# Weight conversion at the start of a top-k attention kernel: the size of each weight written whole to SBUF and multiplied by eight on GpSimd, in place of halves in PSUM that VectorE shifts

## The chip, the cores and the metric

The kernel runs on one core of one Trainium2 chip. The metric is the device time of one execution in microseconds (us); below, "before" is the kernel as it stood and "after" the changed one. The engines are called TensorE (PE in the profile; PEld is its weight load), VectorE (DVE), ScalarE (ACT), GpSimd (POOL) and SyncE (SP), whose queue here issues all DMAs.

## What is computed

Attention that keeps the 32 largest scores of each row, over 8 batches, 8 heads, 576 positions and 64 channels, and behind it a mixer over the positions and channels of each batch:

```python
scores = scale * np.matmul(q, k.transpose(0, 1, 3, 2))
kth = np.partition(scores, -top_k, axis=-1)[..., -top_k:-top_k + 1]
scores = np.where(scores >= kth, scores, -1000000000.0)
attn = np.exp(scores - np.max(scores, axis=-1, keepdims=True))
x = attn / (np.sum(attn, axis=-1, keepdims=True) + 1e-09) @ v      # heads side by side: (8, 576, 512)

theta = x @ w_theta
yr = np.einsum('ts,bsd->btd', w_tok_r, x * np.cos(theta))
yi = np.einsum('ts,bsd->btd', w_tok_i, x * np.sin(theta))
u = x + yr + yi
out = u + np.maximum(u @ w_ch, 0.0)
```

The four weights come as 64-bit floats. The kernel makes 32-bit floats of them itself, and the change is in that step.

## The kernel before

**Work units.** A unit is one tile of 128 query rows of two heads (a pair); each pair has four full units and a half one for the last 64 rows, so a batch has 4 pairs of 5 units and the kernel has 160 units, here counted from 0. A unit goes through these steps. TensorE makes its scores (`ps_score`, from `q2`, `kh`, `kl`). ScalarE copies one part of them to SBUF (`e<-ps_score`). VectorE folds them into a short list (`fold`, `pick`: the tensor_tensor lines on `ps_score`, `lo`, `lst`, and the max lines that write `lst`), finds the 32nd largest in four rounds of max and match_replace (`threshold`), and ends with a small reduce on `best`, called the closing reduce below. GpSimd makes the limit (`lim`), ScalarE a penalty (`pen`), GpSimd subtracts it (`e<-e,pen`, called the subtract below), ScalarE takes the exponent in place, TensorE transposes (`pt`) and multiplies with the values (`px`).

**Mixer.** When a batch is through, its mixer runs piece by piece beside the units of the next batches; the last batch's mixer runs alone at the end.

**Loads of a pair.** `load_pair` fetches `raw`; ScalarE casts it to `hi`, GpSimd makes `raw - hi`, and twelve DMAs lay both out as `q2`, `kh`, `kl` before TensorE can make the first scores of the pair. Pair 0 has a shorter way of its own (`twice`).

**Weights.** `widen_steps` holds 17 conversion jobs: 4 tiles of `w_theta` (128 x 512), 9 of the two token weights (128 x 576), 4 of `w_ch` (128 x 512). A job reads both halves of the 64-bit words by DMA into one of two buffers (`raws`; the DMA of a job waits until the job two before it is through). ScalarE scales the low word into `low`, takes the magnitude of the high word times 2^-112 as a float, and takes its sign in place. The magnitude's bit pattern, shifted left by three, is the bit pattern of the 32-bit float but for its last bits; GpSimd adds `low`, and multiplies by the sign. All of `raws` and `tmps` is one tile, `room`, in the profile. The step "M" of the unit loop emits one job per unit.

**Order.** Code order gives priorities; a scheduler puts all instructions into one queue per engine before the run, with a timeline of its own. Each queue is then worked through strictly in order. So a change of one step can reorder all five queues. Buffers tie the engines together: 11 tiles `e` (also used by `raw` and `hi`), 4 `lst`, 4 `best`, 3 `lim`, 2 score tiles in PSUM.

Of the kernel before, what the change touches and what calls it, by code (L numbers as in the profile page):

```python
# [9 lines left out]
F32 = mybir.dt.float32  # L10
F32R = mybir.dt.float32r
BF16 = mybir.dt.bfloat16
I32 = mybir.dt.int32
U32 = mybir.dt.uint32
AF = mybir.ActivationFunctionType
ALU = mybir.AluOpType
AX = mybir.AxisListType

P = 128
# [27 lines left out]
def topk_attention_phase_mixer(  # L47
# [11 lines left out]
    nc = tc.nc  # L59
    B, NPAIR, _, S = qT.shape  # L60
    DM = w_ch.shape[0]
# [18 lines left out]
    const = ctx.enter_context(tc.tile_pool(name="const", bufs=1))  # L80
# [5 lines left out]
    ps_m = ctx.enter_context(tc.tile_pool(name="ps_m", bufs=2, space=bass.MemoryType.PSUM))  # L86
# [3 lines left out]
    nc.vector.memset(magic, MAGIC)  # L90
    half_pi = const.tile([P, 1], F32, name="half_pi")
    nc.vector.memset(half_pi, HALF_PI)
    warm = const.tile([P, 1], F32, name="warm")
    nc.scalar.activation(warm, magic, AF.Exp, scale=0.0)
    make_identity(nc, ident)
# [20 lines left out]
    def weight_tile(dtype, width):  # L116
        if width == S:
            return wk2.tile([P, S], dtype, tag="w", name="w", bufs=KB + 1)
        return wk2.tile([P, DM], dtype, tag="w5", name="w5", bufs=2 * NB)

    def widen_steps():
        for key, n, width in (("ch", NB, DM), ("th", NB, DM), ("tok", KB, S)):
            wts[key] = [weight_tile(F32, width) for _ in range(n)]
        jobs = []
        for c in range(NB):
            jobs.append((wts["th"][c], (w_theta[c * P : c * P + P],), INV_TWO_PI))
        toks = (w_tok_r, w_tok_i)
        for i, w in enumerate(toks):
            for c in range(NJ):
                jobs.append((wts["tok"][i * NJ + c], (w[c * P : c * P + P],), None))  # L130
        jobs.append((wts["tok"][2 * NJ], [w[NJ * P :] for w in toks], None))
        for c in range(NB):
            jobs.append((wts["ch"][c], (w_ch[c * P : c * P + P],), None))

        room = one.tile([P, ZB * DM], I32, tag="z", name="room")
        raws = [room[:, i * 2 * S : (i + 1) * 2 * S].rearrange("p (n t) -> p n t", t=2) for i in range(2)]
        tmps = [room[:, (i + 2) * 2 * S : (i + 3) * 2 * S].rearrange("p (t n) -> p t n", t=2) for i in range(2)]

        def fetch(i):
            dst, srcs, _ = jobs[i]  # L140
            n = P // len(srcs)
            for k, src in enumerate(srcs):
                nc.sync.dma_start(
                    raws[i % 2][k * n : k * n + n, : dst.shape[-1]],
                    src.bitcast(I32).rearrange("p (n t) -> p n t", t=2),
                )

        def convert(i):
            dst, _, factor = jobs[i]
            n = dst.shape[-1]  # L150
            word, tail = raws[i % 2][:, :n, 1], raws[i % 2][:, :n, 0]
            bits, low = tmps[i % 2][:, 0, :n], tmps[i % 2][:, 1, :n]
            sign = word.bitcast(F32)
            nc.scalar.activation(low, tail.bitcast(U32), AF.Copy, scale=2.0**-29)
            m = n if n <= DM else n // 2
            for c in range(0, n, m):
                size = ps_m.tile([P, 512], F32, tag="m", name="size")[:, :m]
                nc.scalar.activation(size, sign[:, c : c + m], AF.Abs, scale=2.0**-112)
                nc.vector.tensor_scalar(bits[:, c : c + m], size.bitcast(I32), 3, None, op0=ALU.logical_shift_left)
            nc.scalar.activation(sign, sign, AF.Sign)  # L160
            nc.gpsimd.tensor_add(low, low, bits)
            nc.gpsimd.tensor_mul(dst, low.bitcast(F32), sign)
            if factor is not None:
                nc.scalar.mul(dst, dst, factor)

        fetch(0)
        for _ in range(WSTART):
            yield
        for i in range(len(jobs)):
            if i + 1 < len(jobs):  # L170
                fetch(i + 1)
            convert(i)
            yield
# [696 lines left out]
```

## Time and profile before

| | |
|---|---|
| median of 3 runs | 1235.96 us (1234.65 to 1238.25) |
| the profiled execution | 1236.12 us, span 1234.2 us |
| TensorE busy | 1134.4 us, 92% of the span |
| VectorE busy | 1114.9 us, 90% |
| ScalarE busy | 1014.9 us, 82% |
| GpSimd busy | 683.6 us, 55% |
| mean granted TensorE clock | 0.963 |

Busy shares are means over stages with different limits. The weight conversion lies in the first 164 us, in which 20 to 21 of the 160 units and no mixer run.

### The profile page before, as it was taken

What the parts mean: (1) busy time and instruction counts of PE and PEld (TensorE: products, weight loads), DVE (VectorE), ACT (ScalarE), POOL (GpSimd) and SP (SyncE); (2) the same over time, 40 slices, a digit from 0 to 9 for tenths busy, and PEclk for the clock granted to TensorE, in tenths of its full rate; (3) what the DMA queues carried; (4) which work ended last, traced back from release to release, by engine and by line L of the source; (5) the groups of instructions that cost most, each with busy time, mean ns of one, the idle gap of its engine ahead of it and who ended that gap; (6) DMA issues with size and microseconds to landing.
All of it is one profiled execution on the core that took longest, in us unless ns stands there. A gap on an engine that the chain in (4) does not pass through costs nothing.

```text
span 1234.2 us, 22874 instructions
## 1 busy us (share of the span) xinstructions
PE 1134.4 (92%) x6293; PEld 845.6 (69%) x6293; DVE 1114.9 (90%) x5018; ACT 1014.9 (82%) x2098; POOL 683.6 (55%) x958
## 2 busy tenths in 40 slices
PE   4676689799989999999989999999999999999998
PEld 3554456577757876677757777677856777677688
DVE  7999999899999999999999899999999999995353
ACT  4799998998799987898788987898788987888361
POOL 2678873855356553766354654656455654657240
PEclk9776789899999999999999999999999999999999
DMA  6544533333423244333421334233322334200101
GB/s 162 131 131 142 157 90 85 86 87 78 118 64 77 59 107 107 78 90 83 126 63 53 87 97 117 68 96 78 108 68 76 87 97 116 68 19 2 39 2 41
DMA packets 71016, 106.11 MB, mean 86 GB/s; under 512 B 13920, under 2 KB 32608, under 8 KB 70880
## 3 DMA queue, kind: packets, MB, share of 16 engines
q1 hardware_dynamic: 70880, 104.57, 31.9%
q8 instruction: 52, 0.85, 0.3%
q14 instruction: 84, 0.69, 0.2%
HBM read 38.40 MB, written 9.44 MB: 39 GB/s over the span
## 4 chain that ended last, share of the span: by engine, by line
PE 49%; DVE 27%; ACT 16%; issue 3%; DMA 3%; POOL 2%; SPq 1%; ACTq 0%; DVEq 0%; POOLq 0%
PE py L656 18%; PE ps_score L261 7%; PE px L408 7%; PE pt L378 6%; DVE lst L327 5%; DVE best L321 5%; DVE lst L305 5%; PE pth L539 4%; PE po L683 4%; ACT e L363 3%; ACT pen L351 3%; DVE lo L298 3%; ACT e L270 2%; DVE ps_score L297 2%; DVE lst L299 2%
## 5 line engine op out<-in xcount | busy, mean ns | idle before, releaser
L353 POOL TENSOR_TENSOR e<-e,pen 128x576 f32<-128x576 f32 x288 | 365.6, 1284 | 140.0 <-ACT pen L351 137.0
L321 DVE MAX8 best<-lst 128x8 f32<-128x102 f32 (+3 forms) x1152 | 294.5, 310 | 10.8 <-POOL lim L332 10.3
L656 PE MATMUL py<-w,z 128*128 128x288 f32 x1008 | 267.3, 408 | 0.3 <-ACT xt L420 0.3
L363 ACT ACTIVATE e<-e,lim 128x576 f32<-128x576 f32 x288 | 225.0, 782 | 22.3 <-POOL e L353 21.7
L327 DVE MATCH_REPLACE8 lst<-best,lst 128x102 f32<-128x102 f32 (+2 forms) x864 | 241.1, 297 | 0.3 <-issue 0.3
L351 ACT ACTIVATE pen<-e,lim 128x576 bf16<-128x576 f32 x288 | 210.3, 775 | 13.4 <-POOL lim L332 12.9
L305 DVE MAX8 lst<-lo 128x8 f32<-128x72 f32 (+1 forms) x864 | 217.5, 315 | 0.1
L261 PE MATMUL ps_score<-kh,q 128*128 128x288 f32 x512 | 185.0, 376 | 31.0 <-ACT e L270 13.6
L656 PEld LDWEIGHTS py<-w,z 128*128 128x128 f32 x1008 | 182.6, 191 | 40.9 <-ACT xt L420 1.2
L378 PE MATMUL pt<-ident,e 128*128 128x128 f32 x1152 | 183.2, 284 | 26.6 <-ACT e L363 18.8
L378 PEld LDWEIGHTS pt<-ident,e 128*128 128x128 f32 x1152 | 141.7, 145 | 68.6 <-ACT e L363 24.0
L270 ACT COPY e<-ps_score 128x576 f32<-128x576 f32 x256 | 162.1, 641 | 29.4 <-PE ps_score L261 28.1
L380 ACT COPY at<-pt 128x512 f32<-128x512 f32 x256 | 149.7, 588 | 29.3 <-PE pt L378 28.8
L408 PE MATMUL px<-at,vt 128*64 128x320 f32 (+1 forms) x1024 | 166.2, 437 | 1.7 <-ACT at L380 0.4
L261 PE MATMUL ps_score<-kl,q 128*128 128x288 f32 x512 | 151.9, 311 | 0.5 <-DMA kl<-raw 0.5
L261 PEld LDWEIGHTS ps_score<-kh,q 128*128 128x128 f32 x512 | 103.1, 201 | 60.0 <-ACT e L270 24.6
L683 PE MATMUL po<-xt,w 128*128 128x288 f32 x448 | 124.0, 407 | 0.0
L408 PEld LDWEIGHTS px<-at,vt 128*64 128x64 f32 x1024 | 77.5, 145 | 66.1 <-issue 15.5
L298 DVE TENSOR_TENSOR lo<-ps_score,e 128x576 f32<-128x576 f32 (+1 forms) x160 | 113.1, 707 | 0.0
L261 PEld LDWEIGHTS ps_score<-kl,q 128*128 128x128 f32 x512 | 104.1, 203 | 6.8 <-issue 1.9
L539 PE MATMUL pth<-w,xt 128*128 128x512 f32 x224 | 101.6, 596 | 0.2 <-ACT xt L517 0.2
L214 POOL TENSOR_TENSOR raw<-raw,hi 128x1152 fp32r<-128x1152 f32 x31 | 82.1, 2648 | 29.6 <-ACT hi L213 28.2
(130 smaller groups left out, 1924.5 us busy)
## 6 DMA issues: line engine op xcount, KB each, us to landing
kh<-hi SPq DMA_DIRECT2D x124, 144.0 KB, 2.8
kl<-raw SPq DMA_DIRECT2D x124, 144.0 KB, 2.8
raw<-in_qT_dram SPq DMA_DIRECT2D x31, 288.0 KB, 2.9
raw<-in_kT_dram SPq DMA_DIRECT2D x31, 288.0 KB, 3.2
q<-hi SPq DMA_DIRECT2D x62, 144.0 KB, 2.7
q<-raw SPq DMA_DIRECT2D x62, 144.0 KB, 2.9
vt<-in_v_dram SPq DMA_DIRECT2D x32, 256.0 KB, 3.3
out_dram<-ot SPq DMA_DIRECT2D x28, 288.0 KB, 2.3
```

The lines of the kernel that those rows point to most:

```text
L261: nc.tensor.matmul(out[:, at : at + n], l, r, start=(i == 0), stop=(i == len(mm) - 1), skip_group_check=True)
L270: nc.scalar.copy(u.x[:, :, keys], u.ps[:, :, :HS])
L305: nc.vector.max(u.lst[:, w, QS + i * 8 : QS + i * 8 + 8], u.lo1[:, w, lo:hi])
L321: nc.vector.max(top[:, w, best], part[w])
L327: nc.vector.match_replace(out=rest, in_to_replace=top[:, w, best], in_values=part[w], imm_value=LOWEST)
L351: nc.scalar.activation(pen[:, w], u.x[:, w], AF.Relu, bias=u.lim[:, w, 0:1], scale=-STEEP)
L353: nc.gpsimd.tensor_sub(u.x[:, w], u.x[:, w], pen[:, w])
L363: nc.scalar.activation(u.x[:, w], u.x[:, w], AF.Exp, bias=u.lim[:, w, 1:2], scale=SCALE, accum_out=acc)
L378: fixed(nc.tensor.transpose(pt[:, c], e[:, w, at0 : at0 + P], ident))
L408: nc.tensor.matmul(px[sl, :n], pr["vt"][:, kb, sl], pr["at"][:, a, kb], start=(kb == 0), stop=False, skip_group_check=True)
L656: fill(nc.tensor.matmul(py[:, :HS], l, r, start=(i == 0), stop=(i == len(mm) - 1)))
L683: fill(nc.tensor.matmul(po[:, :HS], l, r, start=(i == 0), stop=(i == len(mm) - 1)))
```

## The change

ScalarE's magnitude is written over the whole width straight into `bits` in SBUF: one instruction per job, where there was one into a PSUM tile for the 8 jobs of width 512 and two for the 9 jobs of width 576. The shift by three on VectorE, out of PSUM, is gone; GpSimd multiplies `bits` as 32-bit integers by a column of eights, in place. The column is set once.

```diff
     nc.vector.memset(half_pi, HALF_PI)
+    eight = const.tile([P, 1], I32, name="eight")
+    nc.vector.memset(eight, 8)
     warm = const.tile([P, 1], F32, name="warm")
...
             nc.scalar.activation(low, tail.bitcast(U32), AF.Copy, scale=2.0**-29)
-            m = n if n <= DM else n // 2
-            for c in range(0, n, m):
-                size = ps_m.tile([P, 512], F32, tag="m", name="size")[:, :m]
-                nc.scalar.activation(size, sign[:, c : c + m], AF.Abs, scale=2.0**-112)
-                nc.vector.tensor_scalar(bits[:, c : c + m], size.bitcast(I32), 3, None, op0=ALU.logical_shift_left)
+            nc.scalar.activation(bits.bitcast(F32), sign, AF.Abs, scale=2.0**-112)
+            nc.gpsimd.tensor_tensor(bits, bits, eight.to_broadcast([P, n]), op=ALU.mult)
             nc.scalar.activation(sign, sign, AF.Sign)
             nc.gpsimd.tensor_add(low, low, bits)
             nc.gpsimd.tensor_mul(dst, low.bitcast(F32), sign)
```

The queues are reordered over the first half of the kernel; from about 60% of VectorE's queue on, every queue stands as before. Three places follow.

SyncE's queue at the start, before. The names are the tiles that DMAs write and what they read; `room<-in_w_theta` is the fetch of a conversion job, `raw` the load of pair 1.

```order
L143 DMA room<-in_w_theta_dram 128x1024
L233 DMA vt<-in_v_dram 128x4x128
L236 DMA vrem_95<-in_v_dram 64x64 x2
L143 DMA room<-in_w_theta_dram 128x1024 x2
L189 DMA raw<-in_qT_dram 128x576
L189 DMA raw<-in_kT_dram 128x576
L226 DMA q_265<-hi 64x576
L226 DMA kh<-hi 64x576 x2
```

The same place after (lines are those of the changed file).

```order
L145 DMA room<-in_w_theta_dram 128x1024
L232 DMA vt<-in_v_dram 128x4x128
L235 DMA vrem_97<-in_v_dram 64x64 x2
L145 DMA room<-in_w_theta_dram 128x1024 x3
L188 DMA raw<-in_qT_dram 128x576
L188 DMA raw<-in_kT_dram 128x576
L145 DMA room<-in_w_tok_r_dram 128x1152
L225 DMA q_267<-hi 64x576
L225 DMA kh<-hi 64x576 x2
```

The load of pair 1 stood behind the fetches of jobs 0 to 2; now it stands behind those of jobs 0 to 3, and a fifth fetch stands between it and the DMAs that lay the pair out.

GpSimd's queue at the start, before: L161 is the add of `low`, L162 the multiplication by the sign, L214 the `raw - hi` of pair 1, L353 the subtract of a unit.

```order
L161 TENSOR_TENSOR room<-room 128x512
L162 TENSOR_TENSOR w_238<-room 128x512
L308 COPY marks<-lst 128x2x3 x2
L214 TENSOR_TENSOR raw<-raw,hi 128x1152
L334 COPY marks<-best 128x2x4
L308 COPY marks<-lst 128x2x3
L332 TENSOR_TENSOR lim<-best,factors 128x4
L353 TENSOR_TENSOR e<-e,pen 128x576 x2
```

The same place after; L158 is the new multiplication by eight, L160 the add, L161 the sign, L213 the `raw - hi`.

```order
L158 TENSOR_TENSOR room<-room,eight 128x512
L160 TENSOR_TENSOR room<-room 128x512
L158 TENSOR_TENSOR room<-room,eight 128x512
L161 TENSOR_TENSOR w_240<-room 128x512
L307 COPY marks<-lst 128x2x3
L160 TENSOR_TENSOR room<-room 128x512
L161 TENSOR_TENSOR w_241<-room 128x512
L158 TENSOR_TENSOR room<-room,eight 128x512
L307 COPY marks<-lst 128x2x3
L160 TENSOR_TENSOR room<-room 128x512
L161 TENSOR_TENSOR w_242<-room 128x512
L158 TENSOR_TENSOR room<-room,eight 128x512
```

One job stood ahead of pair 1's `raw - hi`; now three whole jobs and the first multiplication of a fourth do.

GpSimd's queue where the conversions end, before. The numbers tell tiles apart: `e_1479` is unit 18, `w5_237` the last converted weight.

```order
L161 TENSOR_TENSOR room_251<-room_251 128x512
L332 TENSOR_TENSOR lim_1856<-best_1658,factors_91 128x4
L353 TENSOR_TENSOR e_1479<-e_1479,pen_1774 128x576 x2
L334 COPY marks_195<-best_1732 128x2x4
L162 TENSOR_TENSOR w5_237<-room_251 128x512
```

The same place after: `w5_239` is the last converted weight, `e_1033` is unit 13 and `e_1105` unit 14.

```order
L352 TENSOR_TENSOR e_1033<-e_1033,pen_1324 128x576 x2
L333 COPY marks_197<-best_1281 128x2x4
L161 TENSOR_TENSOR w5_238<-room_253 128x512
L158 TENSOR_TENSOR room_253<-room_253,eight_81 128x512
L307 COPY marks_197<-lst_1454 128x2x3
L160 TENSOR_TENSOR room_253<-room_253 128x512
L307 COPY marks_197<-lst_1526 128x3
L331 TENSOR_TENSOR lim_1488<-best_1281,factors_93 128x4
L161 TENSOR_TENSOR w5_239<-room_253 128x512
L352 TENSOR_TENSOR e_1105<-e_1105,pen_1410 128x576
```

The last conversion stood behind the subtract of unit 18; now it stands ahead of that of unit 14.

## Rows read from the trace of the kernel before

**Rows 1.** Stretch, us; busy PE, PEld, DVE, ACT, POOL; granted clock, DMA share, GB/s.

```profile
0.00:62.00 62.00, 33.26 (x134) 25.99 (x135) 53.23 (x236) 40.24 (x75) 27.14 (x43) 0.89 0.56 147
62.00:155.00 93.00, 65.33 (x307) 42.72 (x305) 89.53 (x422) 91.39 (x195) 76.98 (x96) 0.72 0.49 142
310.00:620.00 310.00, 300.95 (x1709) 223.99 (x1708) 301.23 (x1387) 262.21 (x544) 169.44 (x247) 1.00 0.35 90
```

**Rows 2.** VectorE's waits, 62 to 164 us: for whom; us, times, longest.

```profile
DVE ps_score L297 <- ACT e L270: 2.8, 3, 1.0
```

**Rows 3.** Groups by shape, 0 to 164 us: count, busy us, mean ns, idle before.

```profile
L159 DVE TENSOR_SCALAR room<-size 128x288 int32<-128x288 int32 x18 | 8.1, 459 | 0.6 <-ACT size L158 0.6
L159 DVE TENSOR_SCALAR room<-size 128x512 int32<-128x512 int32 x8 | 5.7, 711 | 0.0
...
L158 ACT ACTIVATE size<-room 128x288 f32<-128x288 f32 x18 | 7.8, 442 | 0.0
L160 ACT ACTIVATE room<-room 128x576 f32<-128x576 f32 x9 | 6.9, 770 | 0.1
L160 ACT ACTIVATE room<-room 128x512 f32<-128x512 f32 x8 | 5.6, 694 | 0.0
L158 ACT ACTIVATE size<-room 128x512 f32<-128x512 f32 x8 | 5.2, 645 | 0.0
...
L353 POOL TENSOR_TENSOR e<-e,pen 128x576 f32<-128x576 f32 x35 | 44.3, 1284 | 15.9 <-ACT pen L351 15.9
L161 POOL TENSOR_TENSOR room<-room 128x576 int32<-128x576 int32 x9 | 12.8, 1417 | 3.3 <-DVE room L159 3.2
L161 POOL TENSOR_TENSOR room<-room 128x512 int32<-128x512 int32 x8 | 10.2, 1278 | 13.0 <-DVE room L159 13.0
```

**Rows 4.** VectorE in order of time: start, us, line, operation, shapes.

```profile
11.85 0.47 DVE L297 TENSOR_TENSOR ps_score<-ps_score,e 128x288 f32<-128x288 f32 x1 [1.05 <-ACT e L270]
...
13.39 0.68 DVE L159 TENSOR_SCALAR room<-size 128x512 int32<-128x512 int32 x1
13.99 0.45 DVE L299 TENSOR_TENSOR lst<-ps_score,lo 128x288 f32<-128x288 f32 x1
...
38.72 0.50 DVE L297 TENSOR_TENSOR ps_score<-ps_score,e 128x288 f32<-128x288 f32 x1
...
103.28 0.46 DVE L159 TENSOR_SCALAR room<-size 128x288 int32<-128x288 int32 x1
103.65 0.30 DVE L299 TENSOR_TENSOR lst<-ps_score,lo 128x144 f32<-128x144 f32 x1
...
111.10 0.16 DVE L331 TENSOR_REDUCE best<-best 128x2 f32<-128x8 f32 x1
...
154.98 0.17 DVE L331 TENSOR_REDUCE best<-best 128x2 f32<-128x8 f32 x1
```

**Rows 5.** ScalarE, GpSimd and SyncE's queue in order of time, the start.

```profile
12.28 0.61 ACT L158 ACTIVATE size<-room 128x512 f32<-128x512 f32 x1
...
14.15 1.28 POOL L161 TENSOR_TENSOR room<-room 128x512 int32<-128x512 int32 x1 [12.35 <-DVE room L159]
15.51 1.29 POOL L162 TENSOR_TENSOR w<-room 128x512 f32<-128x512 f32 x1
...
8.97 8.19 SPq L143 DMA_DIRECT2D room<-in_w_theta_dram  x2
17.20 0.43 SPq L189 DMA_DIRECT2D raw<-in_qT_dram  x1
```

**Rows 6.** GpSimd's busy time from 12.9 us to two subtracts, and these.

```profile
12.90:162.61 149.71, 110.49 (x138) 0.77 0.49 138
12.90:110.73 97.83, 65.56 (x83) 0.77 0.46 129
...
109.49 1.28 POOL L353 TENSOR_TENSOR e<-e,pen 128x576 f32<-128x576 f32 x1
160.13 2.55 POOL L353 TENSOR_TENSOR e<-e,pen 128x576 f32<-128x576 f32 x2
```

## The prediction

> **What bounds the kernel now.** I began with the busy time by stage [rows 1], because shares over the whole span say nothing of a step that runs in the first 164 us. From 62 to 155 us VectorE works 89.5 of 93 us and ScalarE 91.4, while TensorE has 65.3 and GpSimd 77.0. Two engines are full at once, and no time is free on either. Before 62 us ScalarE stands idle for 62 - 40.2 = 21.8 us. Later, from 310 to 620 us, VectorE and TensorE both work 301 of 310 us; no conversion is left there. So time saved in the first stage shifts everything behind it, and nothing behind it has idle time into which the gain could leak.
>
> Which of the two full engines leads the first stage? VectorE's waits from 62 us on are 2.8 us, for ScalarE's copies, in three places [rows 2]; otherwise it always finds work. It makes the closing reduce of unit 20 (the 21st) at 155 us, having begun at 11.85 [rows 4]. GpSimd follows: it waits 15.9 us for penalties and 3.2 + 13.0 us for the shift [rows 3], of which 12.35 are the wait for the first one [rows 5].
>
> **VectorE: what goes.** There are 26 shifts, 18 of width 288 and 8 of width 512, with 8.1 + 5.7 = 13.8 us of busy time [rows 3]. Neighbours overlap a little, so I count from start to next start [rows 4]: 103.65 - 103.28 = 0.37 us for the narrow one and 13.99 - 13.39 = 0.60 for the wide. That is 18 x 0.37 + 8 x 0.60 = **11.5 us** that VectorE's queue loses. The column of eights is one memset before VectorE has any work (its first fold starts at 11.85); without that cover it would cost under 0.4 us, the price of a shift 288 wide.
>
> **ScalarE: nearly nothing.** The 26 magnitudes cost 7.8 + 5.2 = 13.0 us [rows 3]. The 17 new ones write SBUF. Width 512 lies between 0.645 us (into PSUM) and 0.694 (the sign, SBUF to SBUF in place); width 576 between 0.70 (0.645 and 64 columns at (0.645 - 0.442) / 224 us each) and 0.770 (the sign). The sum is between 8 x 0.645 + 9 x 0.70 = 11.5 and 8 x 0.694 + 9 x 0.770 = 12.5 us. I take 12.5, since the sign is the nearer row: a gain of 0.5 us, which I leave out of the sum because ScalarE's order changes as well.
>
> The Trainium skill (ScalarE: Activation LUTs, section Step-by-step: what each stage is for) says that ScalarE writes PSUM faster than SBUF, which speaks against this edit. The rows agree for one instruction, 0.645 against 0.694 us at equal width [rows 3]; that would cost 17 x 0.05 = 0.8 us if the count stayed, and by rows the nine fewer instructions outweigh it.
>
> **GpSimd: what comes.** Seventeen integer multiplications, 128 x 512 eight times and 128 x 576 nine times. No row shows a 32-bit integer multiplication or an operand read as a broadcast column. The nearest row is the integer add on the same tiles, 10.2 + 12.8 = **23.0 us** in all [rows 3]. The lower bound is the subtract, 1.284 us at 576 wide (its second operand is half as wide in bytes): 9 x 1.28 + 8 x 1.14 = 20.7. For the upper bound I allow twice the add, 46 us. I take the add: on this engine, operations of different kind on equal tiles differ by a tenth [rows 3].
>
> Is there room for it? GpSimd was busy 110.5 of the 149.7 us from 12.9 us to the end of unit 18's subtract, at 160.13 + 2.55 = 162.7 [rows 6]. In the new queue the same subtract stands behind 17 multiplications more (23.0) and one sign more (1.3): 134.8 us of work. ScalarE's first magnitude ends at 12.28 + 0.61 = 12.9 [rows 5], where GpSimd may start, because it no longer waits for the shift. Without any wait unit 18 then ends at 147.7, 15.0 us earlier than now. In the middle it is tighter. Unit 11's subtract ended at 109.49 + 1.28 = 110.8 [rows 6]; in the new order 14 jobs and one multiplication stand ahead of it, where 9 jobs did: 15 multiplications, 5 adds and 5 signs at about 1.36 and one `raw - hi` at about two subtracts come on top, 36.6 us. 12.9 + 65.6 + 36.6 = 115.1, at best 4.3 us later than now. What covers that lateness is VectorE's lead: it closed unit 13 at 111.1, the 14th closing reduce, only two units ahead of GpSimd [rows 4, 6], and four `best`, four `lst` and eleven `e` tiles let it run some five ahead, at about 6.3 us a unit ((154.98 - 11.85 - 11.5) / 21). If that cover fails, VectorE waits those 4.3 us.
>
> **The start: what is late.** The moved DMAs count here. SyncE's queue is in order, and the second of two fetches held it from 8.97 to 17.16 us, until job 0 left its buffer at 15.51 + 1.29 = 16.8 [rows 5]; right behind it stands pair 1's load, at 17.20. Now a further fetch stands ahead of it, which waits for job 1. GpSimd reaches the end of job 1 after multiply, add, multiply, sign, a small copy, add, sign: from 12.9, four starts 1.24 apart and two dependent ones 1.36 apart (15.51 - 14.15) less the last, the copy 0.15, and 1.29 for the last, about 20.8 us. So pair 1's load moves by 4.0 us, and the cast, the `raw - hi` (now behind three jobs) and the twelve DMAs behind it move too. Pair 1's first fold, now at 38.72 [rows 4], cannot come before about 42.7. VectorE meanwhile has units 0 to 4, some 31 us from 11.85 of which the new order leaves 2 behind that fold: it arrives near 41. That is a stall of 1.7 us, and unit 3's copies, which stand behind two conversions on ScalarE, cost about as much. The bounds are 0 and 4.0 + 2; I take **3 us** lost.
>
> **The sum.** VectorE's queue loses 11.5 us, stalls 3.0 at the start, and I add 2.5 us for new waits between GpSimd's lateness, ScalarE's in-order copies and VectorE: as much again as VectorE's present 2.8 us [rows 2], with bounds 0 and 6. Gain 11.5 - 3.0 - 2.5 = 6.0 us. ScalarE allows it: its 21.8 idle us before 62 take three more theta jobs and several others, since the conversions are now through by unit 14 rather than 18. Against the profiled execution's 1236.1 us (0.2 above the median) this gives **1230 us**. The bounds of the terms give 1224.6 (nothing lost) to 1236 (all lost), and the reordered middle of the kernel can add a microsecond or two either way, as VectorE and TensorE are both full there.
>
> **Rivals.** 0.3% of the time, 3.7 us, is about what can be told from no change here.
>
> *GpSimd becomes the bound (slower).* It needs one thing: an integer multiplication dearer than the add. Its place is GpSimd's queue from 12.9 us to the last conversion, which now stands ahead of unit 14. Each 0.1 us on its price costs 1.7 us there. The room is 15.0 us less the waits that remain; of GpSimd's present 149.7 - 110.5 = 39.2 idle us most are waits for engines that lead; an engine that is last keeps few of them, and I reckon 5. From 10 / 17 = 0.6 us over the add's 1.35, that is about 1.95 us, the stage is no shorter than before. At twice the add it is 23.0 - 10 = 13 us longer: 1249. For it speaks that no row shows the operation; against it, that add, subtract and sign cost nearly the same.
>
> The Trainium skill (GPSIMD Engine Reference, section 4.1, engine selection) puts elementwise work on VectorE, GpSimd being about twice as slow with two inputs. The trace agrees, 1.278 us for the add against 0.711 for the shift at width 512 [rows 3]; if that alone decided, the change would lose, and it is this rival.
>
> *ScalarE is the bound (no change).* It is fuller than VectorE from 62 us on [rows 1] and its own work hardly changes. Then VectorE's 11.5 us become waits for copies, and only ScalarE's 0.5 us and a little of the early filling come through: 1233 to 1236. Against it: VectorE hardly ever waits for it now [rows 2], and the new order uses its early idle time.
>
> *The whole saving comes through.* No stall at the start, no new waits: 1224.
>
> **How the numbers follow.** Forecast (1224.5 to 1232.3): 0.50. Whole saving or better: 0.03. No change, within 3.7 us: 0.25. GpSimd as the bound, above 1239.8: 0.22. Faster is 0.53. For eight in ten I leave out the best case and the upper half of the slow one: 1224 to 1246; the forecast's own range is 1224 to 1234.
>
> **What the profile after would show.** The multiplication's mean against 1.28 and 1.42 us, and GpSimd's busy time 23 us up; a mean of 2 us or more makes the prediction wrong. Pair 1's first fold near 42 to 43 us. Unit 18's subtract ending near 150 to 156. The 21st closing reduce near 149. VectorE's waits between 62 and 164 us under 6 us; if they are 10 or more and name ScalarE's copies, the second rival holds. Behind 310 us the stages should keep their length; if the gain at 155 us is there and the end is not earlier, it was given back in the reordered middle.

## The result and the profile after

| | before | after |
|---|---|---|
| median | 1236.03 us (1234.65 to 1238.25, 5 runs) | 1225.36 us (1224.60 to 1227.21, 5 runs) |
| ratio, with 95% interval | | 0.9911 [0.9897, 0.9926] |
| span of the profiled execution | 1234.2 us | 1223.5 us |

The change made the kernel 10.7 us faster; the prediction said 6. The page of the changed kernel, busy time of each engine, its share and its instructions:

```profile
PE 1129.3 (92%) x6293; PEld 844.0 (69%) x6293; DVE 1103.5 (90%) x4993; ACT 1017.0 (83%) x2089; POOL 700.6 (57%) x975
```

VectorE has 11.4 us less to do (1114.9 before), GpSimd 17.0 more (683.6), ScalarE 2.1 more. The stages, which answer to [rows 1] (stretch; busy PE, PEld, DVE, ACT, POOL; granted clock, DMA share, GB/s):

```profile
0.00:62.00 62.00, 30.84 (x132) 25.44 (x133) 51.70 (x241) 48.81 (x92) 46.79 (x64) 0.86 0.67 181
62.00:155.00 93.00, 71.37 (x339) 49.56 (x339) 89.82 (x439) 89.00 (x182) 82.20 (x101) 0.71 0.48 133
...
310.00:620.00 310.00, 300.74 (x1703) 222.18 (x1702) 297.70 (x1366) 261.28 (x540) 165.87 (x241) 1.00 0.34 90
```

Up to 155 us VectorE is as busy as before (141.5 us against 142.8), although 11 us of shifts are gone: that time now holds work on units. Before 62 us ScalarE does 8.6 us more and GpSimd 19.7 us more, the conversions that the new order starts earlier. The groups by shape of the first 164 us, which answer to [rows 3] (count, busy us, mean ns, idle before):

```profile
L158 POOL TENSOR_TENSOR room<-room,eight 128x576 int32<-128x576 int32 x9 | 10.3, 1148 | 0.0
L160 POOL TENSOR_TENSOR room<-room 128x512 int32<-128x512 int32 x8 | 10.2, 1277 | 0.2
L158 POOL TENSOR_TENSOR room<-room,eight 128x512 int32<-128x512 int32 x8 | 8.3, 1044 | 16.4 <-ACT room L157 16.4
L159 ACT ACTIVATE room<-room 128x576 f32<-128x576 f32 x9 | 6.8, 757 | 0.0
L157 ACT ACTIVATE room<-room 128x576 f32<-128x576 f32 x9 | 6.6, 734 | 0.0
...
L157 ACT ACTIVATE room<-room 128x512 f32<-128x512 f32 x8 | 5.3, 665 | 0.0
```

The multiplication by a column is cheaper than the add, 1044 ns against 1277 at width 512; all 17 cost 18.6 us. VectorE's waits from 62 to 164 us, which answer to [rows 2]:

```profile
DVE ps_score L296 <- ACT e L269: 3.2, 5, 1.5
```

Four places in order of time, which answer to [rows 4 to 6]: pair 1's load in SyncE's queue, pair 1's first fold, the 21st closing reduce, and the subtract of which unit 18's is the second half:

```profile
8.96 11.85 SPq L145 DMA_DIRECT2D room<-in_w_theta_dram  x3
20.86 0.43 SPq L188 DMA_DIRECT2D raw<-in_qT_dram  x1
...
41.64 0.47 DVE L296 TENSOR_TENSOR ps_score<-ps_score,e 128x288 f32<-128x288 f32 x1 [1.38 <-ACT e L269]
...
149.72 0.17 DVE L330 TENSOR_REDUCE best<-best 128x2 f32<-128x8 f32 x1
...
154.07 2.54 POOL L352 TENSOR_TENSOR e<-e,pen 128x576 f32<-128x576 f32 x2 [0.46 <-ACT pen L350]
```

Pair 1's load is 3.7 us later and VectorE stalls 1.4 us at its first fold. The 21st closing reduce is 5.3 us earlier. Only later does the lead grow: the closing reduce of unit 25 comes 11.6 us earlier than before, that of unit 40 15.9, of unit 50 14.3, and the end 10.7. Single closings swing with the order (unit 35's comes only 4.0 us earlier), so they place the gain roughly: about a half of it appears behind the stage that was changed. Over the whole span VectorE's idle time is nearly the same, 1223.5 - 1103.5 = 120.0 us against 1234.2 - 1114.9 = 119.3.

### The profile page after: what moved, and what is told of

It is laid out like the page before. It is cut to its first block, busy times and chain, and to the rows that moved or that the text cites. A ratio compares the mean times of both kernels' runs of the same rounds, so it can differ in the third digit from the quotient of the medians.

```text
span 1223.5 us, 22890 instructions
## 1 busy us (share of the span) xinstructions
PE 1129.3 (92%) x6293; PEld 844.0 (69%) x6293; DVE 1103.5 (90%) x4993; ACT 1017.0 (83%) x2089; POOL 700.6 (57%) x975
## 4 chain that ended last, share of the span: by engine, by line
PE 48%; DVE 28%; ACT 15%; issue 3%; POOL 3%; DMA 2%; SPq 1%; ACTq 0%; DVEq 0%; POOLq 0%
PE py L655 17%; PE ps_score L260 6%; PE px L407 6%; DVE best L320 5%; PE pt L377 5%; DVE lst L326 5%; DVE lst L304 5%; PE pth L538 5%; PE po L682 4%; ACT e L362 3%; DVE lo L297 3%; ACT pen L350 3%; ACT e L269 2%; DVE ps_score L296 2%; DVE lo L296 2%
## 5 line engine op out<-in xcount | busy, mean ns | idle before, releaser
L320 DVE MAX8 best<-lst 128x8 f32<-128x102 f32 (+3 forms) x1152 | 287.1, 297 | 15.6 <-POOL lim L331 15.1
L326 DVE MATCH_REPLACE8 lst<-best,lst 128x102 f32<-128x102 f32 (+2 forms) x864 | 235.0, 284 | 0.0
L260 PE MATMUL ps_score<-kh,q 128*128 128x288 f32 x512 | 182.3, 371 | 45.7 <-ACT e L269 23.1
L304 DVE MAX8 lst<-lo 128x8 f32<-128x72 f32 (+1 forms) x864 | 213.5, 302 | 0.0
L377 PEld LDWEIGHTS pt<-ident,e 128*128 128x128 f32 x1152 | 141.5, 145 | 68.4 <-ACT e L362 25.1
L407 PE MATMUL px<-at,vt 128*64 128x320 f32 (+1 forms) x1024 | 161.8, 425 | 3.4 <-ACT at L382 1.7
L213 POOL TENSOR_TENSOR raw<-raw,hi 128x1152 fp32r<-128x1152 f32 x31 | 82.1, 2648 | 32.6 <-ACT hi L212 30.9
```

The source lines that it names most:

```text
L260: nc.tensor.matmul(out[:, at : at + n], l, r, start=(i == 0), stop=(i == len(mm) - 1), skip_group_check=True)
L304: nc.vector.max(u.lst[:, w, QS + i * 8 : QS + i * 8 + 8], u.lo1[:, w, lo:hi])
L320: nc.vector.max(top[:, w, best], part[w])
L326: nc.vector.match_replace(out=rest, in_to_replace=top[:, w, best], in_values=part[w], imm_value=LOWEST)
L377: fixed(nc.tensor.transpose(pt[:, c], e[:, w, at0 : at0 + P], ident))
L407: nc.tensor.matmul(px[sl, :n], pr["vt"][:, kb, sl], pr["at"][:, a, kb], start=(kb == 0), stop=False, skip_group_check=True)
```

## The experiments

The theories. Theory 1: the gain is VectorE's saved time, less what new waits take, and GpSimd has the room for the multiplications. Its rivals, stated in the expectations where they are tried, give other parts of the change a share: ScalarE's instructions, the start, and GpSimd's load, which by Theory 4 has a price that adds to that of VectorE's. Theory 5 came last, when the first eight runs gave no sum: every edit changes the durations that the scheduler reckons with, and the new order of the queues has a worth of its own. Ratios are to the kernel before, run on the same chip.

**The shift back on VectorE, but in SBUF.**

```diff
-            nc.gpsimd.tensor_tensor(bits, bits, eight.to_broadcast([P, n]), op=ALU.mult)
+            nc.vector.tensor_scalar(bits, bits, 3, None, op0=ALU.logical_shift_left)
```

> ScalarE writes the magnitude whole to SBUF as in the changed kernel, but VectorE shifts it there in place (17 shifts of full width) and GpSimd multiplies nothing. Theory 1 (the gain is the time that left VectorE's queue): 17 shifts out of SBUF cost 8 x 0.60 + 9 x 0.66 = 10.7 us at the rate of the old ones, so about 1235 us; if VectorE shifts faster out of SBUF, the time is 1225.4 plus the new shifts' time less 1. Theory 2 (the gain is ScalarE's: one whole write in place of halves, and no PSUM tile taken from the mixing step): 1225 to 1228 us, with GpSimd's added work gone as well.

Measured: 1231.70 us, 0.9964 [0.9952, 0.9977]; 3 us faster than expected, though VectorE has as much to do as before. It also showed something of the hardware: these shifts take 404 to 2218 ns, where those out of PSUM took 443 to 753 at their two widths. In order of time, this kernel's VectorE and GpSimd about one long shift and one short of it:

```profile
55.17 0.62 DVE L304 MAX8 lst<-lo 128x8 f32<-128x72 f32 x4
55.71 2.22 DVE L158 TENSOR_SCALAR room<-room 128x576 int32<-128x576 int32 x1
57.85 0.08 DVE L326 MATCH_VALUE_LOAD lst<-best,lst 128x8 f32 x1
...
54.97 2.64 POOL L213 TENSOR_TENSOR raw<-raw,hi 128x1152 fp32r<-128x1152 f32 x1
...
72.26 1.06 DVE L158 TENSOR_SCALAR room<-room 128x576 int32<-128x576 int32 x1
...
71.73 1.28 POOL L352 TENSOR_TENSOR e<-e,pen 128x576 f32<-128x576 f32 x1
```

Each began while a GpSimd instruction ran (to 57.61 and to 73.01) and ended 0.31 to 0.32 us after it, at 57.93 and 73.32, however long that took. Nine of the 17 shifts began while a GpSimd instruction ran, and all nine ended 0.28 to 0.34 us after it; of the 26 shifts out of PSUM in the kernel before, 17 began in the same way, and ten of these ended before the GpSimd instruction did. So a shift from SBUF to SBUF waits here for GpSimd to finish. The Trainium skill (SBUF — State Buffer, section Who interferes with whom) says that such an operation of VectorE can take a pair of ports that GpSimd shares, and that the one that comes second then stands still for the whole instruction; these rows agree. From start to next start these shifts cost VectorE 11.3 us, as those out of PSUM did; why the kernel is 4 us faster than before all the same, with the load where it was, this run does not tell (its order too is another).

**VectorE's load put back beside the change.** 26 shifts of the column of eights into a spare PSUM tile, as many and as wide as before; nobody reads them.

```diff
+            m = n if n <= DM else n // 2
+            for c in range(0, n, m):
+                spare = ps_m.tile([P, 512], F32, tag="m", name="spare")[:, :m]
+                nc.vector.tensor_scalar(
+                    spare.bitcast(I32), eight.to_broadcast([P, m]), 3, None, op0=ALU.logical_shift_left
+                )
```

> The changed kernel with the 26 old VectorE shifts put back as load alone: they shift the column of eights, read as a broadcast, into the PSUM tile that the size once used, and nobody reads it. Theory 1 expects the gain to go: 11.5 us on VectorE's queue, 1234 to 1238 us. Theory 2 expects 1225 to 1229 us, since ScalarE's and GpSimd's work are those of the changed kernel.

Measured: 1235.67 us, 0.9995 [0.9986, 1.0004]. The gain is gone, as Theory 1 says. But the scheduler had reordered the queues again (the added shifts left out, only the first 204 and the last 82 of VectorE's 4,993 instructions run in the changed kernel's sequence, by the traces), so this run alone does not tell load from order.

**More, dearer and no multiplications on GpSimd.** Twice the multiplications, by two and by four:

```diff
-    nc.vector.memset(eight, 8)
+    nc.vector.memset(eight, 2)
+    four = const.tile([P, 1], I32, name="four")
+    nc.vector.memset(four, 4)
...
+            nc.gpsimd.tensor_tensor(bits, bits, four.to_broadcast([P, n]), op=ALU.mult)
```

> The changed kernel with two multiplications on GpSimd, by two and by four, in place of one by eight: 17 more at 1.04 and 1.15 us, 18.6 us more on GpSimd ahead of unit 14. If GpSimd is already the bound of the stage: plus 16 to 19, 1242 to 1244 us. If its lateness is still covered by VectorE's lead: 1225 to 1227 us. Theory 1 expects something between, plus 3 to 8, 1228 to 1233 us: unit 11's subtract is 7 us later than in the kernel before as it is, and would be some 20 later, about the lead that the buffers allow.

Measured: 1230.42 us, 0.9949 [0.9933, 0.9964], 5 us more than the change; GpSimd is then busy 90.3 of the 93 us from 62 to 155. The order is one of its own here too.

The full low word as second operand in place of the column:

```diff
-            nc.gpsimd.tensor_tensor(bits, bits, eight.to_broadcast([P, n]), op=ALU.mult)
+            nc.gpsimd.tensor_tensor(bits, bits, low, op=ALU.mult)
```

> The changed kernel with GpSimd multiplying by the low word, a full tile, in place of the column of eights, so that the output is not the reference's; it prices the operation. If the column read as a broadcast makes the multiplication cheap: 1.28 and 1.41 us, as the add, GpSimd 4.3 us busier, 1225 to 1227 us. If an integer multiplication is itself cheaper than an add: 1.04 and 1.15 us, 1225 us. If it is dearer on a full tile, as the rival of the prediction had it: 2 us or more.

Measured: 1232.96 us, 0.9965 [0.9950, 0.9981], 7.6 us more than the change, for 4.6 us more of GpSimd. The groups of that kernel:

```profile
L158 POOL TENSOR_TENSOR room<-room 128x576 int32<-128x576 int32 x9 | 12.9, 1429 | 2.8 <-ACT room L157 2.8
L158 POOL TENSOR_TENSOR room<-room 128x512 int32<-128x512 int32 x8 | 10.3, 1283 | 15.8 <-ACT room L157 15.8
```

That is the add's price: it is the column, not the multiplication, that made the changed kernel's 1044 and 1148 ns. The time of the whole kernel says less, because its queues too are in another order than the changed kernel's.

The multiplication left out:

```diff
-            nc.gpsimd.tensor_tensor(bits, bits, eight.to_broadcast([P, n]), op=ALU.mult)
```

> The changed kernel without the multiplication by eight: the shift is left out altogether, so that the weights are not the reference's. GpSimd loses 18.6 us. Theory 4 expects GpSimd's term back: 1220 to 1222 us. Theory 1 expects 1224 to 1226 us, since GpSimd's lateness is covered by VectorE's lead.

Measured: 1239.95 us (1234.23 to 1245.11 over 12 runs), 1.0025 [1.0010, 1.0040]: 14.6 us slower than the change, with 18.6 us less on GpSimd and no instruction more on any engine. No theory of loads gives that sign: Theory 4 falls, and the order came into question.

A multiplication by one added to the kernel before, behind the shift:

```diff
+            nc.gpsimd.tensor_tensor(bits, bits, unit1.to_broadcast([P, n]), op=ALU.mult)
```

> The kernel before, with halves in PSUM and VectorE's shift, and on GpSimd a multiplication by one of the shifted tile, of the new one's shape, ahead of the add. GpSimd's load grows by 18.6 us and nothing else changes. Theory 4 expects GpSimd's term: plus 4 to 5, 1240 to 1241 us. Theory 1 expects 1235 to 1237 us: while VectorE leads, GpSimd has the room.

Measured: 1237.59 us, 1.0010 [1.0000, 1.0021]. In the kernel before, 18.6 us more of GpSimd cost about 1 us (the kernel before had 1236.54 beside it), in an order that is again another.

**The start, and ScalarE in halves.** Conversions told to begin four steps later:

```diff
-WSTART = 2
+WSTART = 6
```

> The changed kernel with the conversions beginning four units later in the code order (WSTART 6 for 2), so that they may not fill the first 62 us to the same extent. Theory 1 expects 1223 to 1228 us: VectorE's work is the same, and the small stall at the load of pair 1 can go. Theory 3 (the gain comes from conversions that fill ScalarE's and GpSimd's idle time at the start and are through by unit 14): 1229 to 1233 us.

Measured: 1224.73 us, 0.9911 [0.9895, 0.9927]. The scheduler made the very same five queues of it, so it says nothing of the start; it is a second measurement of the change, with the same ratio.

The 576-wide magnitudes written in two halves, as before, but to SBUF:

```diff
-            nc.scalar.activation(bits.bitcast(F32), sign, AF.Abs, scale=2.0**-112)
+            m = n if n <= DM else n // 2
+            for c in range(0, n, m):
+                nc.scalar.activation(bits[:, c : c + m].bitcast(F32), sign[:, c : c + m], AF.Abs, scale=2.0**-112)
```

> The changed kernel, but ScalarE writes the magnitude of the nine 576-wide jobs in two halves again, to SBUF: nine instructions more, some 0.1 us each of real time. Theory 4 (three terms that add: VectorE's queue -11 us, ScalarE's whole write and the freed PSUM tile -4, GpSimd's multiplication +4.5) expects 1226 to 1229 us if the number of ScalarE's instructions carries its -4, and 1225 if the PSUM tile does. Theory 1 expects 1225 to 1226.5 us.

Measured: 1237.28 us, 1.0004 [0.9992, 1.0015]. With nine more short instructions on ScalarE the whole gain is gone, 12 us, where 1225 to 1229 was expected. The order is another one here too: by the traces, the first 212 and the last 704 of VectorE's 4,993 instructions run in the changed kernel's sequence, and those between do not. So this run does not show that the instructions themselves cost the gain.

**The load put back, the order kept.** To part load from order, the queues of the changed kernel were made first, and then 26 reductions were set into VectorE's finished queue, behind every twentieth instruction from the 60th on. All rows of the five queues stand as in the changed kernel.

```diff
+    made = [
+        nc.vector.tensor_reduce(
+            held[:, 1 + i : 2 + i], held[:, :1].to_broadcast([128, WIDE]), axis=mybir.AxisListType.X, op=mybir.AluOpType.max
+        ).ins
+        for i in range(LOADS)
+    ]
...
+    for i, x in reversed(list(zip(seat, made))):
+        main.instructions.insert(i, x)
```

> The changed kernel with its order kept word for word on all five engines: behind every twentieth VectorE instruction, from its 60th on, one reduction over 352 columns into a column that nobody reads is set in, 26 in all, after the order had been fixed; none waits and none is waited for. They should take about 0.43 us each, 11 us together, as much as the 26 shifts did, and end before 150 us. Theory 1 (the gain is VectorE's saved time, which bounds the kernel): the time goes up by 9 to 12 us, to 1234 to 1238. Theory 5 (the gain is the other order that the scheduler made of the same work, not the time that VectorE saves): it goes up by under 4 us, to 1225 to 1229.

Measured: 1229.77 us (1228.01 to 1231.07), 0.9948 [0.9935, 0.9961]: 4.4 us more than the change, between the two expectations; the last reductions ran at 161 us, later than the 150 that was expected. The group, the page's line and VectorE's waits up to 164 us of this kernel:

```profile
L843 DVE TENSOR_REDUCE held<-held x26: 510/566/609, 26.1 to 161.2; 128x1 f32<-128x352 f32 x26
```

```profile
PE 1131.7 (92%) x6293; PEld 845.0 (69%) x6293; DVE 1113.8 (91%) x5020; ACT 1015.6 (83%) x2089; POOL 700.7 (57%) x975
```

```profile
DVE kl L206 <- ACT kh L205: 5.9, 1, 5.9
DVE ps_score L296 <- ACT e L269: 1.1, 1, 1.1
DVE q L209 <- ACT q L208: 0.9, 1, 0.9
```

The load is back (busy time 10.3 us up; start to next start, the 26 take 11.0 us, 0.42 for one). In the changed kernel the same list has 5.7 us for the copies, in seven places:

```profile
DVE ps_score L296 <- ACT e L269: 5.7, 7, 1.5
```

So of 10.3 us that VectorE was relieved of at this order, 5.7 - 1.1 = 4.6 us turned into waits for ScalarE's copies, and 4.4 us came through to the end; the remaining 1.3 us are not placed.

What the other 6 us are is read from two kernels with nearly the same work, the two with the load put back, one in the scheduler's order for it (1235.67) and one in the changed kernel's (1229.77); VectorE's busy time is 1115.4 us in the first and 1113.8 in the second. Their stages, the first of the scheduler's own order:

```profile
62.00:155.00 93.00, 64.07 (x314) 43.88 (x313) 88.65 (x409) 85.04 (x178) 78.53 (x96) 0.76 0.42 120
155.00:217.00 62.00, 51.38 (x268) 36.14 (x269) 59.96 (x276) 49.73 (x107) 30.03 (x48) 0.89 0.33 82
217.00:310.00 93.00, 89.22 (x494) 67.56 (x493) 87.21 (x416) 83.59 (x174) 60.47 (x85) 0.96 0.35 86
310.00:620.00 310.00, 301.17 (x1713) 224.77 (x1712) 301.23 (x1382) 262.05 (x546) 169.67 (x247) 1.00 0.35 91
sum 620.00, PE 538.10 PEld 398.05 DVE 589.58 ACT 529.18 POOL 385.08; mean PE 107.62 PEld 79.61 DVE 117.92 ACT 105.84 POOL 77.02
```

and of the order kept:

```profile
62.00:155.00 93.00, 69.66 (x323) 47.56 (x322) 93.00 (x444) 85.54 (x176) 81.26 (x99) 0.71 0.44 126
155.00:217.00 62.00, 51.82 (x280) 34.49 (x279) 61.78 (x280) 56.51 (x121) 34.84 (x54) 0.94 0.29 77
217.00:310.00 93.00, 90.33 (x521) 70.34 (x520) 89.59 (x430) 82.99 (x175) 57.14 (x85) 1.00 0.33 84
310.00:620.00 310.00, 300.90 (x1703) 222.81 (x1703) 297.41 (x1358) 261.60 (x542) 166.24 (x243) 1.00 0.34 92
sum 620.00, PE 543.57 PEld 400.00 DVE 594.95 ACT 535.15 POOL 385.67; mean PE 108.71 PEld 80.00 DVE 118.99 ACT 107.03 POOL 77.13
```

In the sums, which include the stage before 62 us, VectorE gets 594.95 - 589.58 = 5.4 us more done in the first 620 us: 8.5 us more from 62 to 310, where it is busy 244.4 of 248 us, and 3.8 less behind 310. That is about the 5.9 us between the two. From 62 to 310 us VectorE stands idle 12.2 us in the scheduler's own order and 3.6 in the order kept, and most of the difference is waits for ScalarE's copies, in the first and in the second:

```profile
DVE ps_score L302 <- ACT e L275: 7.9, 6, 2.6
...
DVE ps_score L296 <- ACT e L269: 1.4, 3, 0.7
```

Two other causes can be looked for in these runs. The 26 shifts of the first kernel write PSUM tiles of the pool that also serves `px`, and the reductions do not; but no instruction of the trace waited for one of these shifts, and none of the shifts waited. The granted clock does not tell the two apart either: the means of their runs are 0.961 to 0.975 and 0.962 to 0.977.

**The pair in an order made without durations.** The scheduler can also order without a timeline. The idea was that the two kernels would then have nearly one order.

```diff
-    with _tile.TileContext(nc, schedule_with_timeline_sim=True) as tc:
+    with _tile.TileContext(nc, schedule_with_timeline_sim=False) as tc:
```

> The kernel before, ordered without the scheduler's modelled durations. Such orders of the two kernels are the same behind the start but for the edit itself (2,287 VectorE rows in one piece and 306 in another stand alike in both), so that the pair compares the change at almost one order. The time itself is unknown: 1235 to 1300.

> The changed kernel, ordered in the same way. Theory 1: 7 to 13 us faster than the kernel before in that order. Theory 5: within 4 us of it.

> The changed kernel in that order, with GpSimd's multiply left out, so that the widened weights are not the reference's. GpSimd has 17 instructions less, 18.6 us. If GpSimd has the room (Theory 1), it is within 3 us of the changed kernel in that order, and the 14.6 us that the same edit cost in the scheduler's timed order were that order's. If the multiply's time lies on the path (Theory 4), it is 4 us or more faster. If it is slower by 10 us again, the loss is not the order's, and the multiply's delay itself helps.

Measured: before 1448.97 us, 1.1758 [1.1723, 1.1793]; after 1462.60, 1.1830 [1.1813, 1.1847]; without the multiplication 1453.42, 1.1770 [1.1748, 1.1793]. The expectations of before and after missed: here the same edit costs 13.6 us by the medians (9 by the ratios). It is no control for the gain: by the traces, VectorE's last 4,177 instructions run in the same sequence in both, but the 841 and 816 ahead of them, among which the conversions lie, do not. What it shows is where such an order loses. The first 217 us and the next 1183 of the kernel before:

```profile
0.00:217.00 217.00, 133.88 (x596) 94.55 (x597) 169.01 (x761) 164.62 (x335) 124.55 (x164) 0.81 0.42 115
217.00:1400.00 1183.00, 1104.40 (x5428) 749.47 (x5426) 954.74 (x4229) 853.51 (x1747) 559.80 (x791) 0.99 0.26 67
```

and after:

```profile
0.00:217.00 217.00, 127.14 (x519) 88.74 (x520) 147.08 (x696) 154.03 (x302) 138.61 (x176) 0.80 0.42 111
217.00:1400.00 1183.00, 1104.70 (x5434) 749.65 (x5432) 957.21 (x4256) 854.70 (x1752) 555.48 (x790) 0.99 0.27 68
```

Behind 217 us TensorE, the fullest engine there, is equally busy. Before it, VectorE gets 21.9 us less done, more than the 11 it is relieved of. Up to 217 us its waits for ScalarE were 11.8 us for copies and 17.5 for magnitudes; now there are no magnitudes to wait for, and the waits for copies are

```profile
DVE ps_score L296 <- ACT e L269: 50.6, 14, 12.5
```

Without the multiplication VectorE is busy 157.4 us in that stretch and the time is 9.2 us less, 7.4 by the ratios (by the traces, all but 30 of VectorE's 4,993 instructions run in the same sequence). That is what Theory 4 expected of this run. So in this order GpSimd's 18.6 us do lie on the path, by about half; and leaving them out helps. The 14.6 us that the same edit cost in the timed order are then hardly the missing instructions' doing; the order made for it is what is left, though that edit was not run with the changed kernel's order kept.

## Why the prediction was right, and where it was not

**The bound and VectorE's 11.5 us: right.** Busy time fell by 11.4. The first stage is led by VectorE: with the load back and the order kept the 21st closing reduce stands at 155.2 us, as before at 154.98, and without the load at 149.7; near 149 was predicted.

**The losses, 3.0 at the start and 2.5 of new waits: near in sum at the kept order, too large beside the kernel before.** At the kept order, copies cost VectorE 4.6 us that they don't cost with the load back (1.5 before 62 us, 3.2 behind it, rounded); predicted were 5.5. The stall at pair 1's first fold was 1.38 us for 1.7, the fold came at 41.64 for 42 to 43. The prediction counted from the kernel before. There the waits for copies were 1.05 us at the start [rows 4] and 2.8 behind it [rows 2], so that the 5.7 us after are only 1.8 more. At the kept order 4.4 us come through at the end and 5.5 at the 21st closing reduce, near the predicted 6.0. The prediction also said that nothing behind the first stage has idle time into which the gain could leak; from 310 to 620 us VectorE is busy 297.7 us after, for 301.2 before, so 3.5 us of idle time came there.

**ScalarE: right to leave out.** The 17 magnitudes cost 11.9 us for 13.0, between the bounds 11.5 and 12.5; at width 512 one took 0.665 us into SBUF, for 0.645 into PSUM.

**GpSimd's 23.0 us: too dear by 4.4.** Measured 18.6, under the lower bound of 20.7, since the nearest rows all had a full second operand and the new one reads a column. Unit 18's subtract ended at 156.6, just behind the 150 to 156 of the text, and unit 11's at 117.8 for at best 115.1. VectorE's lead covered that, as said: no row of its waits up to 164 us names GpSimd. The rival with GpSimd as the bound needed 1.95 us an instruction and got 1.09. The 1.278 and 0.711 us that it set side by side are an add of two tiles and a shift of one, so they do not compare the two engines at the same operation. With the multiplications doubled the time was 5 us more, and with 18.6 us of GpSimd added to the kernel before about 1; both kernels had orders of their own, so these are not prices of the load alone.

**The step that failed: "the reordered middle of the kernel can add a microsecond or two either way".** That term was mis-sized. With VectorE's load in both, the order made for the change is worth 5.9 us against the one made for the same kernel with its load back, and 6.1 against the kernel before. Other orders of nearly the same work stood at 1237.28 and 1239.95, 12 and 15 us from the change. So on the path that was run, first the new order and then the relief, the gain of 10.7 us is about 6 us of a luckier order and 4.4 of relief. That the time came out near the forecast, on the better side, is in part luck: in the kernel at 1237.28, with nine more short instructions and another order, the same relief showed no gain. Of the kernels here, those made without a timeline aside, the five with VectorE's shifts or a load in their place lie between 1229.77 and 1237.59 us and the six without between 1224.73 and 1239.95: unless the order is held, such times do not tell what the relief is worth.

**What stays open.** The split of 6 and 4.4 holds for that one path. What the relief is worth in the order of the kernel before was not measured. Read from before and after alone, VectorE has 11.4 us less to do and 0.7 more of idle time, which would be the account of the rival in which the whole saving (1224) comes through; against that rival stand the stall of 1.38 us at the start and the 4.6 us of waits at the kept order. That the kept order waits less for copies from 62 to 310 us is shown; which row's move brings it is not. The 6.1 us against the kernel before also hold whatever GpSimd gained by not waiting for VectorE's shift (16.2 us in [rows 3]); the 5.9 us between the two kernels with the load put back don't have that part, which speaks against a large one. An order of before with the shifts taken out of its finished queue was not tried, because the add needs what they write.

## What to carry to other kernels

Relieving the leading engine of 11 us gave about 4 at a fixed order: the engine behind it in the loop, here ScalarE with its copies, took most of the rest as new waits. Where a scheduler orders the queues by modelled durations, every edit is two edits, and the second, the new order, can be worth as much or more with either sign; set the load into the finished queues, or compare kernels of equal work in several orders, before a gain is put down to an engine. An edit that is slower than it should be, as the one that only left instructions out, is a sign to look at the order first.

## What the hardware showed that was not expected

- GpSimd's 32-bit integer multiplication takes 1.04 us at 128 x 512 and 1.15 at 128 x 576 with a column as second operand, 1.28 and 1.43 with a full one, where the integer add takes 1.28 and 1.41; here the second operand makes the price, not the operation.
- A VectorE shift from SBUF to SBUF that meets a running GpSimd instruction ends 0.3 us after that one, up to 2.2 us in all; out of PSUM, in other widths, the shifts stayed within 0.44 to 0.75.
